# A decode kernel's load order: w_gate first, into a free slot of the key ring, ahead of wq, the first keys and w_up

## The chip, the cores and the metric

One Trainium2 chip, one core. The metric is the device time of one execution in microseconds (us), the median of a few runs: 377.54 us for the kernel before (three runs, 377.37 to 377.6). All tensors are float32. Engines are written as in the profile: PE (TensorE), PEld (its weight loads), DVE (VectorE), ACT (ScalarE), POOL (GpSimd), SP (SyncE, which issues nearly all transfers here).

## What is computed

One token is normalised and goes through two blocks in parallel, attention over a cache of 32 heads x 4096 keys x 128, and a gated feed-forward (FFN) block whose hidden width is 1376:

```
xn = layernorm(x)                                   # 1 x 512
q  = xn @ wq                                        # 32 heads x 128
p  = softmax(q . k_cache * 128**-0.5)               # per head, 4096 keys
A  = (p @ v_cache) @ wo
h  = silu(xn @ w_gate) * (xn @ w_up)                # 1376 wide
B  = xn + (h @ w_down) * sigmoid(xn . w_r)
out = x + A + B
```

The sizes follow from the shapes: wq 8.39 MB, w_gate and w_up 2.82 MB each, k_cache and v_cache 67.1 MB each, wo 8.39 MB, w_down 2.82 MB.

## The kernel before

The 32 heads go in `NG = 8` groups of four. The keys of a group (8.39 MB, 128 partitions x 16384 values) take two of the three slots of `ring` (`SLOT` = 8192 values a partition), the values of a group fill `vals` (two slots wide). The loop at L392 handles, in turn g, the scores of group g and the softmax and the product with the values of group g-1.

- **Keys.** `load_keys` (L99) puts group g into slots 2g mod 3 and the next one, in one transfer, or in two where the ring wraps. K0 takes slots 0 and 1; K1 slot 2 (its first half, here K1a) and slot 0 (K1b); K2 slots 1 and 2.
- **Scores.** DVE multiplies keys by the query (`multiply`, L241) and adds up (`sums`, L251); POOL does the last 24 of 64 rows of each half (`rest`, L256 and L258). The sums of a half free its slot.
- **Softmax.** `own_max` (L304 to L308), `head_max` (L313), `expo` (L321, then POOL L323).
- **Values.** 32 products on PE per group (`values`, L332), two records each in the profile.
- **Queue.** All large transfers are issued by SP, in program order, each behind its own waits. The data then flows in that order.

What stands ahead of the loop matters here. SP loads wq into `vals` (L81) and K0 into the ring (L96). PE makes the query (L217, then L230), ACT copies it (L222, L233). When the products of wq have read the front of `vals`, w_gate and w_up are loaded there (L89, called at L225). DVE and POOL start on K0 (L273 to L275). PE multiplies w_gate into the PSUM bank `ps_acc` and w_up into `ps_o` (`ffn_in`, L261, called at L276). `gate` and `up` are used only after the values of group 0 (`ffn_hidden`, L278). The values of group 0 (V0) overwrite `vals` (L395), so SP waits for the products of w_up.

Of the kernel before, what the change touches and what calls it, by code (L numbers as in the profile page):

```python
# [20 lines left out]
NCOL = 4  # L21
# [6 lines left out]
def kernel(  # L28
# [13 lines left out]
    nc = tc.nc  # L42
    _, H, Sk, Dh = k_cache.shape
    D = x.shape[-1]
    F = w_gate.shape[1]
    NK = D // P
# [10 lines left out]
    FL = F - FM  # L57
    FC = FM // NCOL
    QC = QB * Dh
    HC = C // 2  # L60
    SLOT = HC * Dh
# [15 lines left out]
    ring = const.tile([P, SLOTS * SLOT], F32, name="ring")  # L77
    vals = const.tile([P, 2 * SLOT], F32, name="vals")

    def load_wq(t):  # L80
        nc.sync.dma_start(t, wq.rearrange("(p j) n -> p (j n)", p=P))  # L81

        return [
            t[:, j * H * Dh:(j + 1) * H * Dh].rearrange("p (b h k n) -> p b h k n", b=NB, h=HP, n=QC)
            for j in range(NK)
        ]

    def load_in(t, w):
        nc.sync.dma_start(t, w.rearrange("(p j) f -> p (j f)", p=P))  # L89
        return [t[:, j * F:(j + 1) * F] for j in range(NK)]  # L90
# [8 lines left out]
    def load_keys(g):  # L99

        i = 2 * g % SLOTS * SLOT
        if i + 2 * SLOT <= SLOTS * SLOT:
            t = load_group(k_cache, g, ring[:, i:i + 2 * SLOT])
            return t[:, :HC], t[:, HC:]
        return load_group(k_cache, g, ring[:, i:]), load_group(k_cache, g, ring[:, :SLOT], HC)
# [19 lines left out]
    xr, wr, xn, row = (rows[0:1, i].rearrange("o g d -> o (g d)") for i in range(G))  # L125
    nc.scalar.dma_start(xr, x[0])
    nc.scalar.dma_start(wr, w_r.rearrange("(o n) -> o n", o=1))
    WQ = load_wq(vals)
    K, V = {0: load_keys(0)}, {}

# [8 lines left out]
    ps_acc = ps_1.tile([P, 512], F32, name="ps_acc")  # L139
    ps_o = ps_1.tile([P, 512], F32, name="ps_o")  # L140
# [45 lines left out]
    ps = ps_s.tile([P, 512], F32, name="ps_small")  # L186
    for j in range(NK):
        nc.tensor.matmul(ps[:, j:j + 1], xn.rearrange("o (p j) -> o j p", j=NK)[:, j], ones[0:1, 0:1],  # L188
                         start=True, stop=True)
    xnT = const.tile([P, NK], F32, name="xnT")  # L190
# [13 lines left out]
    ps = ps_s.tile([P, 512], F32, name="ps_small")  # L204
# [5 lines left out]
    nc.vector.tensor_tensor(base, base, xr, op=ALU.add)  # L210


    NR = NQ * HP // NCOL
    for j in range(NK):
        for i in range(NQ * HP):
            t, k = i % NCOL, i // HP
            nc.tensor.matmul(ps_pv[i // NCOL][32 * t:32 * t + 1, :QC], xnT[:, j:j + 1],  # L217
                             WQ[j][:, k * QB // GB, i % HP, k % (GB // QB), :],
                             start=(j == 0), stop=(j == NK - 1), skip_group_check=True)
    q_sb = const.tile([P, NR, QC], F32, name="q_sb")  # L220
    for i in range(NR):
        nc.scalar.activation(q_sb[:, i, :], ps_pv[i][:, :QC], AF.Copy)  # L222


    W_GATE, W_UP = (load_in(vals[:, i * NK * F:(i + 1) * NK * F], w) for i, w in enumerate((w_gate, w_up)))  # L225

    def q_part(k):

        ps = ps_q.tile([P, QB, Dh], F32, name="q")
        nc.tensor.matmul(ps.rearrange("p g d -> p (g d)"), pick.rearrange("p i h -> p (i h)"), q_sb[:, k, :],  # L230
                         start=True, stop=True)

        nc.scalar.activation(q_sb[:, k, :], ps.rearrange("p g d -> p (g d)"), AF.Copy)  # L233
        return ps
# [11 lines left out]
    def sums(g, i):  # L246
        if i == 0:
            S[g] = small.tile([P, C], F32, name="s")
        k, s = K[g][i], S[g][:, i * HC:(i + 1) * HC]
        for c, n in ((slice(0, HC - NP), Dh), (slice(HC - NP, HC), Dh // 2)):  # L250
            nc.vector.tensor_reduce(s[:, c], k[:, c, :n], axis=AX.X, op=ALU.add)  # L251
# [6 lines left out]
        nc.gpsimd.tensor_tensor(a, a, b, op=ALU.add)  # L258


    def ffn_in(W, ps):  # L261

        for j in range(NK):
            for t in range(NCOL):
                a = FL if t else 0
                nc.tensor.matmul(ps[32 * t:32 * t + 1, a:FL + FC], xnT[:, j:j + 1],  # L266
                                 W[j][:, a + t * FC:FL + (t + 1) * FC],
                                 start=(j == 0), stop=(j == NK - 1), skip_group_check=True)
        return ps[:, :FL + FC]

    Q = {0: q_part(0)}

    rest(0, 0)  # L273
    multiply(0, 0, 0, HC - NP)
    sums(0, 0)  # L275
    gate, up = ffn_in(W_GATE, ps_acc), ffn_in(W_UP, ps_o)  # L276

    def ffn_hidden():  # L278

# [112 lines left out]
    for g in range(NG + 1):  # L392
# [3 lines left out]
        elif g:  # L396

            i = 2 * g % SLOTS * SLOT
# [42 lines left out]
    for j in range(NCOL):  # L441
        nc.tensor.matmul(fin(j), ones[0:1, 0:1], base[:, j * DC:(j + 1) * DC],
                         start=True, stop=False, skip_group_check=True)
# [39 lines left out]
```

## Time and profile before

| what | value |
|---|---|
| median of three runs | 377.54 us |
| the profiled execution, its own time | 377.8 us |
| its span, first to last instruction | 375.9 us |
| read from HBM | 159.52 MB, 424 GB/s over the span |
| DMA queue of SP and its packets, share of 16 engines | 98.3% |
| busy share PE / DVE / ACT / POOL | 31% / 61% / 4% / 46% |
| granted PE clock, mean | 0.681 |

The profiled execution took 0.26 us more than the median; its time lies 1.9 us above its span. A "landing" below is the moment at which an engine that waited for a transfer starts. The issue row of a transfer says when SP handed it to the queue, not when its data began to flow.

### The profile page before, as it was taken

What the parts mean: (1) busy time and instruction counts of PE and PEld (TensorE: products, weight loads), DVE (VectorE), ACT (ScalarE), POOL (GpSimd) and SP (SyncE); (2) the same over time, 40 slices, a digit from 0 to 9 for tenths busy, and PEclk for the clock granted to TensorE, in tenths of its full rate; (3) what the DMA queues carried; (4) which work ended last, traced back from release to release, by engine and by line L of the source; (5) the groups of instructions that cost most, each with busy time, mean ns of one, the idle gap of its engine ahead of it and who ended that gap; (6) DMA issues with size and microseconds to landing.
All of it is one profiled execution on the core that took longest, in us unless ns stands there. A gap on an engine that the chain in (4) does not pass through costs nothing.

```text
span 375.9 us, 2047 instructions
## 1 busy us (share of the span) xinstructions
PE 116.5 (31%) x846; PEld 34.4 (9%) x846; DVE 230.8 (61%) x124; ACT 15.6 (4%) x36; POOL 171.5 (46%) x52
## 2 busy tenths in 40 slices
PE   1155063000810072006300580045002700181994
PEld 1111011000200020001100130011000200020222
DVE  6300599999468990799699105994399699500010
ACT  3001000000010000100100000000000000010001
POOL 2000496992008940795696004970399299000000
PEclk9999557555785578555855596559555855586799
DMA  8999899999999899999999899999998999999994
GB/s 335 446 446 446 386 435 443 446 446 446 440 439 425 384 441 446 446 432 398 443 485 425 384 448 446 446 425 441 439 446 387 418 458 439 446 420 404 436 420 199
DMA packets 4190, 159.64 MB, mean 425 GB/s; under 512 B 467, under 2 KB 467, under 8 KB 854
## 3 DMA queue, kind: packets, MB, share of 16 engines
q1 hardware_dynamic: 4178, 159.52, 98.3%
q8 instruction: 6, 0.10, 0.1%
q14 instruction: 2, 0.02, 0.0%
q10 hardware_dynamic: 4, 0.00, 0.0%
HBM read 159.52 MB, written 0.00 MB: 424 GB/s over the span
## 4 chain that ended last, share of the span: by engine, by line
DMA 79%; PE 20%; issue 0%; SPq 0%; ACTq 0%; ACT 0%; DVE 0%
DMA vals<-in_A_v_cache_dram 57%; PE ps_pv L332 17%; DMA ring<-in_A_wo_dram 9%; DMA vals<-in_B_w_up_dram 7%; DMA vals<-in_A_wq_dram 6%; PE ps_pv L217 2%; PE ps_o L266 1%; PE ps_acc L388 0%; SPq L112 0%; PE ps_small L308 0%; ACTq L478 0%; ACT res L451 0%; DVE nm L313 0%; PE ps_o L388 0%
## 5 line engine op out<-in xcount | busy, mean ns | idle before, releaser
L256 POOL TENSOR_TENSOR ring<-ring,q_sb 128x3072 f32<-128x3072 f32 x16 | 106.9, 6679 | 147.3 <-DMA ring<-in_A_k_cache_dram 147.3
L241 DVE TENSOR_TENSOR ring<-ring,q 128x2560 f32<-128x2560 f32 (+1 forms) x23 | 88.7, 3857 | 83.2 <-DMA ring<-in_A_k_cache_dram 83.2
L332 PE MATMUL ps_pv<-vals,pt 128*16 128x512 f32 x448 | 62.5, 721 | 185.6 <-DMA vals<-in_A_v_cache_dram 185.6
L251 DVE TENSOR_REDUCE s<-ring 128x40 f32<-128x5120 f32 (+1 forms) x32 | 114.3, 3614 | 0.8
L258 POOL TENSOR_TENSOR ring<-ring 128x1536 f32<-128x1536 f32 x16 | 55.0, 3435 | 1.3
L332 PEld LDWEIGHTS ps_pv<-vals,pt 128*16 128x16 f32 x448 | 14.9, 111 | 228.3 <-issue 228.3
L323 POOL TENSOR_TENSOR pt<-e,mine 128x512 f32<-128x512 f32 x8 | 8.3, 1042 | 17.7 <-ACT e L321 17.7
L341 ACT ACTIVATE pv<-ps_pv 128x512 f32<-128x512 f32 x8 | 4.8, 597 | 215.0 <-PE ps_pv L332 215.0
L332 PE MATMUL ps_pv<-ring,pt 128*16 128x512 f32 x64 | 9.4, 754 | 10.1 <-DMA ring<-in_A_v_cache_dram 10.1
L357 DVE RECIPROCAL rinv<-ps_small 128x4 f32<-128x4 f32 x2 | 0.4, 178 | 19.7 <-PE ps_small L348 19.7
L217 PE MATMUL ps_pv<-vals,xnT 128*1 128x512 f32 x64 | 9.2, 739 | 10.4 <-DMA vals<-in_A_wq_dram 10.4
L266 PE MATMUL ps_acc<-vals,xnT 128*1 128x320 f32 (+1 forms) x32 | 5.7, 772 | 15.6 <-DMA vals<-in_B_w_gate_dram 15.6
L313 DVE TENSOR_REDUCE nm<-ps_small 128x1 f32<-128x32 f32 x8 | 1.5, 184 | 11.8 <-PE ps_small L308 11.8
L308 PE MATMUL ps_small<-dg,same 128*128 128x32 f32 x16 | 3.6, 309 | 14.5 <-DVE dg L306 14.5
L350 PE MATMUL ps_o<-pv,first 128*128 128x512 f32 x16 | 7.4, 605 | 0.8 <-ACT pv L341 0.8
L321 ACT ACTIVATE e<-s,nm 128x128 f32<-128x128 f32 x8 | 3.2, 402 | 98.4 <-DVE nm L313 98.4
L453 DVE COPY res<-ps_acc 1x128 f32<-1x128 f32 x2 | 0.6, 281 | 10.9 <-PE ps_o L388 10.9
L306 DVE TENSOR_SCALAR dg<-fold,m 128x32 f32<-128x32 f32 x8 | 6.6, 820 | 0.3
L196 DVE TENSOR_SCALAR hid<-hid 128x416 f32<-128x416 f32 x1 | 0.4, 377 | 7.1 <-ACT hid L195 7.1
L308 PEld LDWEIGHTS ps_small<-dg,same 128*128 128x128 f32 x16 | 2.9, 218 | 20.1 <-issue 18.2
L188 PE MATMUL ps_small<-ones,pv 1*128 1x1 f32 x8 | 2.0, 370 | 8.3 <-DVE pv L184 8.3
L359 DVE TENSOR_TENSOR o<-ps_o,rinv 128x512 f32<-128x512 f32 x2 | 2.1, 1064 | 4.0 <-PE ps_o L350 3.9
(88 smaller groups left out, 70.3 us busy)
## 6 DMA issues: line engine op xcount, KB each, us to landing
ring<-in_A_k_cache_dram SPq DMA_DIRECT2D x6, 4096.0 KB, 35.2
vals<-in_A_wo_dram SPq DMA_DIRECT2D x1, 4096.0 KB
vals<-in_B_w_gate_dram SPq DMA_DIRECT2D x1, 2752.0 KB, 20.9
vals<-in_B_w_up_dram SPq DMA_DIRECT2D x1, 2752.0 KB, 25.9
vals<-in_B_w_down_dram SPq DMA_DIRECT2D x1, 2560.0 KB
ring<-in_A_wo_dram SPq DMA_DIRECT2D x1, 2048.0 KB, 31.1
ring<-in_A_wo_dram SPq DMA_DIRECT2D x1, 1024.0 KB, 33.2
ring<-in_A_wo_dram SPq DMA_DIRECT2D x1, 768.0 KB, 34.5
```

Of the source, the lines that this page charges most:

```text
L217: nc.tensor.matmul(ps_pv[i // NCOL][32 * t:32 * t + 1, :QC], xnT[:, j:j + 1], WQ[j][:, k * QB // GB, i % HP, k % (GB // QB), :], start=(j ...
L241: nc.vector.tensor_tensor(k[:, c0:c1, :], k[:, c0:c1, :], q[:, None, :].to_broadcast([P, c1 - c0, Dh]), op=ALU.mult)
L251: nc.vector.tensor_reduce(s[:, c], k[:, c, :n], axis=AX.X, op=ALU.add)
L256: nc.gpsimd.tensor_tensor(k, k, q[:, None, :].to_broadcast([P, NP, Dh]), op=ALU.mult)
L258: nc.gpsimd.tensor_tensor(a, a, b, op=ALU.add)
L266: nc.tensor.matmul(ps[32 * t:32 * t + 1, a:FL + FC], xnT[:, j:j + 1], W[j][:, a + t * FC:FL + (t + 1) * FC], start=(j == 0), stop=(j == NK ...
L306: nc.vector.tensor_scalar(dg, fold, m, SCALE, op0=ALU.mult, op1=ALU.mult)
L308: nc.tensor.matmul(ps[:, :PP], same.rearrange("p i h -> p (i h)"), dg, start=True, stop=True)
L323: nc.gpsimd.tensor_tensor(PT[g % 2], e[:, :, None].to_broadcast([P, C, HP]), mine[:, None, :].to_broadcast([P, C, HP]), op=ALU.mult)
L332: nc.tensor.matmul(ps[r:r + M, :], p[:, G * i:G * (i + 1), :].rearrange("p c h -> p (c h)"), v[:, G * i:G * (i + 1), :].rearrange("p c d - ...
L341: nc.scalar.activation(PV[g // GB][:, :, g % GB, :], ps_pv[g % 2].rearrange("p (c d) -> p c d", c=G), AF.Copy)
L350: nc.tensor.matmul(ps_o, first[:, c].rearrange("p h i -> p (h i)"), pv[:, c].rearrange("p k d -> p (k d)"), start=(c == 0), stop=(c == G - 1))
```

## The change

w_gate is loaded by the first instruction on SP, into slot 2 of the ring, which K1a needs only later. Its products are issued on PE before those of wq. `ffn_in` moves up for that, and w_up alone takes the front of `vals`.

```
+    W_GATE = load_in(ring[:, 2 * SLOT:2 * SLOT + NK * F], w_gate)
     WQ = load_wq(vals)
     K, V = {0: load_keys(0)}, {}
...
+    def ffn_in(W, ps):        # the body is unchanged, moved up from behind rest()
...
+    gate = ffn_in(W_GATE, ps_acc)
     NR = NQ * HP // NCOL
     for j in range(NK):       # the products of wq
...
-    W_GATE, W_UP = (load_in(vals[:, i * NK * F:(i + 1) * NK * F], w) for i, w in enumerate((w_gate, w_up)))
+    W_UP = load_in(vals[:, :NK * F], w_up)
...
     sums(0, 0)
-    gate, up = ffn_in(W_GATE, ps_acc), ffn_in(W_UP, ps_o)
+    up = ffn_in(W_UP, ps_o)
```

How it moves instructions on SP, the issuing engine, at the start of the program (a row is one transfer, destination, source and shape; x2 is two transfers, K1a and K1b). Before:

```order
L81 DMA vals<-in_A_wq_dram 128x16384
L96 DMA ring<-in_A_k_cache_dram 128x1x16384
L89 DMA vals<-in_B_w_gate_dram 128x5504
L89 DMA vals<-in_B_w_up_dram 128x5504
L96 DMA ring<-in_A_k_cache_dram 128x1x8192 x2
L96 DMA vals<-in_A_v_cache_dram 128x1x16384
```

Now:

```order
L89 DMA ring<-in_B_w_gate_dram 128x5504
L81 DMA vals<-in_A_wq_dram 128x16384
L96 DMA ring<-in_A_k_cache_dram 128x1x16384
L89 DMA vals<-in_B_w_up_dram 128x5504
L96 DMA ring<-in_A_k_cache_dram 128x1x8192 x2
L96 DMA vals<-in_A_v_cache_dram 128x1x16384
```

One transfer moved from third place to first, past wq and K0. From w_up on the order is what it was, to the end of the program.

And on PE, at the start of the program (the first rows of w_gate and of wq, the last of wq, the query and what follows). Before:

```order
L205 MATMUL ps_small<-rp,ones 128x1
L217 MATMUL ps_pv_94<-vals,xnT 1x512 x4
...
L217 MATMUL ps_pv_95<-vals,xnT 1x512 x4
L230 MATMUL q<-q_sb,pick 128x512
L266 MATMUL ps_acc<-vals,xnT 1x416
L266 MATMUL ps_acc<-vals,xnT 1x320 x3
...
L266 MATMUL ps_o<-vals,xnT 1x416
```

Now:

```order
L206 MATMUL ps_small<-rp,ones 128x1
L219 MATMUL ps_acc<-ring,xnT 1x416
L219 MATMUL ps_acc<-ring,xnT 1x320 x3
...
L229 MATMUL ps_pv_96<-vals,xnT 1x512 x4
L242 MATMUL q<-q_sb,pick 128x512
L219 MATMUL ps_o<-vals,xnT 1x416
```

The 16 products into `ps_acc` (32 records in the profile) moved from behind the query to ahead of the products of wq. The orders of DVE, ACT and POOL are the same in both kernels.

## Rows read from the trace of the kernel before

**Rows 1.** The page: the span; the shares of the chain that ended last, by engine; two DMA queues with packets, MB and the time of their packets as a share of 16 engines' span.

```profile
span 375.9 us, 2047 instructions
...
q1 hardware_dynamic: 4178, 159.52, 98.3%
q8 instruction: 6, 0.10, 0.1%
...
DMA 79%; PE 20%; issue 0%; SPq 0%; ACTq 0%; ACT 0%; DVE 0%
```

**Rows 2.** The chain of waits in order of time, five of its 81 pieces: start, us, what.

```profile
30.38 25.91 DMA vals<-in_B_w_up_dram
...
56.34 3.02 PE ps_o L266 x28
...
59.37 35.55 DMA vals<-in_A_v_cache_dram
...
104.06 29.48 DMA vals<-in_A_v_cache_dram
...
337.61 34.52 DMA ring<-in_A_wo_dram
```

**Rows 3.** Timeline of SP's queue: start, us, the transfer that was issued. In order: wq, K0, w_gate, w_up, K1a, K1b, V0, K2.

```profile
0.74 0.40 SPq L81 DMA_DIRECT2D vals<-in_A_wq_dram  x1
1.20 0.61 SPq L96 DMA_DIRECT2D ring<-in_A_k_cache_dram  x1
27.82 0.33 SPq L89 DMA_DIRECT2D vals<-in_B_w_gate_dram  x1
30.38 0.33 SPq L89 DMA_DIRECT2D vals<-in_B_w_up_dram  x1
30.76 0.55 SPq L96 DMA_DIRECT2D ring<-in_A_k_cache_dram  x1
...
54.95 0.54 SPq L96 DMA_DIRECT2D ring<-in_A_k_cache_dram  x1
59.37 0.54 SPq L96 DMA_DIRECT2D vals<-in_A_v_cache_dram  x1
...
85.48 0.53 SPq L96 DMA_DIRECT2D ring<-in_A_k_cache_dram  x1
```

**Rows 4.** Timeline of PE up to 70 us: start, us, what, and in brackets the idle time before it and what ended it.

```profile
11.93 0.58 PE L205 MATMUL ps_small<-rp,ones 1*128 1x1 f32 x2 [1.56 <-DVE rp L203]
22.89 9.17 PE L217 MATMUL ps_pv<-vals,xnT 128*1 128x512 f32 x64 [10.38 <-DMA vals<-in_A_wq_dram]
...
48.72 5.71 PE L266 MATMUL ps_acc<-vals,xnT 128*1 128x416 f32 x32 [15.60 <-DMA vals<-in_B_w_gate_dram]
56.34 2.95 PE L266 MATMUL ps_o<-vals,xnT 128*1 128x416 f32 x32 [1.91 <-DMA vals<-in_B_w_up_dram]
```

**Rows 5.** Timeline of DVE from K0's landing to the end of K1's sums, the next instruction after them, and a later instruction of the kind of `dg`.

```profile
42.25 5.49 DVE L241 TENSOR_TENSOR ring<-ring,q 128x5120 f32<-128x5120 f32 x1 [27.86 <-DMA ring<-in_A_k_cache_dram]
47.77 7.15 DVE L251 TENSOR_REDUCE s<-ring 128x40 f32<-128x5120 f32 x2
...
67.53 0.29 DVE L304 TENSOR_REDUCE m<-s 128x1 f32<-128x128 f32 x1
67.85 4.87 DVE L306 TENSOR_SCALAR dg<-fold,m 128x32 f32<-128x32 f32 x1
72.63 2.81 DVE L241 TENSOR_TENSOR ring<-ring,q 128x2560 f32<-128x2560 f32 x1
...
78.30 7.14 DVE L251 TENSOR_REDUCE s<-ring 128x40 f32<-128x5120 f32 x2
...
90.88 7.15 DVE L251 TENSOR_REDUCE s<-ring 128x40 f32<-128x5120 f32 x2
105.10 0.38 DVE L196 TENSOR_SCALAR hid<-hid 128x416 f32<-128x416 f32 x1 [7.08 <-ACT hid L195]
...
110.73 0.24 DVE L306 TENSOR_SCALAR dg<-fold,m 128x32 f32<-128x32 f32 x1
```

**Rows 6.** Timeline of POOL: the first instruction on K0, the last on K0, the first on K1a.

```profile
42.30 6.68 POOL L256 TENSOR_TENSOR ring<-ring,q_sb 128x3072 f32<-128x3072 f32 x1 [39.51 <-DMA ring<-in_A_k_cache_dram]
...
59.27 3.43 POOL L258 TENSOR_TENSOR ring<-ring 128x1536 f32<-128x1536 f32 x1
66.03 6.65 POOL L256 TENSOR_TENSOR ring<-ring,q_sb 128x3072 f32<-128x3072 f32 x1 [3.33 <-DMA ring<-in_A_k_cache_dram]
```

**Rows 7.** Timeline of PEld in the slow first part of the products of wq (start of each four weight loads), and of ACT at the last copy of the query.

```profile
23.70 0.15 PEld L217 LDWEIGHTS ps_pv<-vals,xnT 128*1 128x1 f32 x4 [0.70 <-issue]
24.55 0.15 PEld L217 LDWEIGHTS ps_pv<-vals,xnT 128*1 128x1 f32 x4 [0.70 <-issue]
...
33.16 0.60 ACT L233 ACTIVATE q_sb<-q 128x512 f32<-128x512 f32 x1 [0.42 <-PE q L230]
```

**Rows 8.** Stretches of time: length, busy time of PE, PEld, DVE, ACT, POOL (count), granted PE clock (1.00 is 2.4 GHz, 0.50 is 1.2 GHz), DMA share, GB/s.

```profile
2.00:4.00 2.00, 0.00 (x0) 0.00 (x0) 1.85 (x9) 0.81 (x1) 0.70 (x3) 1.00 0.60 229
4.00:6.00 2.00, 0.00 (x0) 0.00 (x0) 1.83 (x7) 0.00 (x0) 0.00 (x0) 1.00 1.21 524
...
50.00:52.00 2.00, 2.00 (x19) 0.70 (x15) 2.00 (x1) 0.00 (x0) 2.00 (x1) 0.50 1.12 484
...
56.00:58.00 2.00, 1.66 (x26) 0.81 (x30) 2.00 (x1) 0.00 (x0) 2.00 (x1) 1.00 0.87 377
```

More of the change, by code (lines that the diff above doesn't have):

```diff
@@ L127 @@
     nc.scalar.dma_start(wr, w_r.rearrange("(o n) -> o n", o=1))
+    W_GATE = load_in(ring[:, 2 * SLOT:2 * SLOT + NK * F], w_gate)
     WQ = load_wq(vals)
@@ L210, with ffn_in @@
     nc.vector.tensor_tensor(base, base, xr, op=ALU.add)
+    def ffn_in(W, ps):
+        for j in range(NK):
+            for t in range(NCOL):
+                a = FL if t else 0
+                nc.tensor.matmul(ps[32 * t:32 * t + 1, a:FL + FC], xnT[:, j:j + 1],
+                                 W[j][:, a + t * FC:FL + (t + 1) * FC],
+                                 start=(j == 0), stop=(j == NK - 1), skip_group_check=True)
+        return ps[:, :FL + FC]
+    gate = ffn_in(W_GATE, ps_acc)
     NR = NQ * HP // NCOL
@@ L222 @@
         nc.scalar.activation(q_sb[:, i, :], ps_pv[i][:, :QC], AF.Copy)
-    W_GATE, W_UP = (load_in(vals[:, i * NK * F:(i + 1) * NK * F], w) for i, w in enumerate((w_gate, w_up)))
+    W_UP = load_in(vals[:, :NK * F], w_up)
     def q_part(k):
@@ L258, in rest @@
         nc.gpsimd.tensor_tensor(a, a, b, op=ALU.add)
[L261 to L269, printed above, removed]
     Q = {0: q_part(0)}
@@ L275 @@
     sums(0, 0)
-    gate, up = ffn_in(W_GATE, ps_acc), ffn_in(W_UP, ps_o)
+    up = ffn_in(W_UP, ps_o)
     def ffn_hidden():
```

## The prediction

> **What bounds the kernel now.** I read the page first, then the chain of waits, then the timelines of the queue and of the engines that wait for it. The chain puts 79% on DMA and 20% on PE [rows 1], which looks as if products of PE stood between the transfers. Among its pieces are those of w_up, after which V0 is issued [rows 2]. But SP's queue has its packets in flight for 98.3% of the span [rows 1], so such a product can delay the *issue* of a transfer and not its data. The chain shows it: V0 takes 35.55 us from issue to landing and V1 29.48 [rows 2]. V0 was simply issued earlier into a full queue.
>
> So I measured the flow between landings. K0 lands 19.36 us after wq (22.89 to 42.25) [rows 4, 5], 8.39 MB at 433 GB/s. w_gate follows after 6.47 us (to 48.72) [rows 4], 2.82 MB at 436. w_up takes 7.62 (to 56.34), 1.15 more than w_gate for the same bytes. K1a takes 9.69 (to 66.03) [rows 6], 4.19 MB at 433. K1b and V0 take 28.89 (to 59.37 + 35.55 = 94.92) [rows 2], 12.58 MB at 435. K2 and V1 take 38.62 (to 104.06 + 29.48 = 133.54) [rows 2], 16.78 MB at 434. The rate is the same whatever the tensor. The first transfer alone takes 22.89 us where 19.36 would be its flow, so 3.53 us pass at the start. Over the whole kernel: 3.53 + 1.15 + 159.52 MB at 434.5 GB/s (367.1) = 371.8; the last transfer lands at 337.61 + 34.52 = 372.13 [rows 2]. Start, bytes and a tail of 3.8 us make the span. A change of order can only act through the start, or by a gap in the queue.
>
> **The change part by part.** Nothing is added or removed: the same transfers, the same products. Three things move.
>
> *w_gate's transfer goes ahead of wq and K0.* By the flow, w_gate lands at 3.53 + 6.47 = 10.0, wq at 29.36 (6.47 later than before), K0 at 48.72 (6.47 later). w_up then lands at 56.34 and K1a at 66.03 as before, since the bytes ahead of them are the same. The issue of w_gate takes SP 0.33 us [rows 3]; wq and K0 are issued that much later, hidden behind the 6.47 us in which w_gate flows. If the step of 1.15 us that w_up shows comes before K0's end now, K0 lands at 49.87. I carry 48.72 and keep 49.87 as the upper bound.
>
> *w_gate's products go ahead of those of wq.* PE is idle from 12.51 to 22.89 [rows 4], and in the new order until 29.36. 32 records cost 5.71 us at a granted clock of 0.50 (w_gate) or 2.95 at 1.00 (w_up) [rows 4, 8], so they end by 18.3. Queued behind them are the products of wq, due at 29.36: not delayed. K1a, which needs the slot, is issued much later.
>
> *What comes later, and when each would leave the queue dry.* The trace has no transfer issued into an empty queue except the first. That one took 22.15 us from issue (0.74) to landing [rows 3, 4] against 19.36 behind another, so it must be issued at most 2.79 us before its data is due. Zero is the other bound; I take 2.79, the only row there is.
>
> - w_up waits for the front of `vals`, 4.93 us into the products of wq (22.89 to 27.82, where w_gate's issue stands now) [rows 3, 4], so it is issued at 34.3. If PE ran slow throughout (0.85 us for four of 64 loads [rows 7], 6.8 us for that half), 36.2. Due by 48.72 - 2.79 = 45.9. Hidden.
> - The query is ready at 33.76 [rows 7], 10.87 after wq's landing; now 40.2, or 44.7 if all 64 loads go slowly (13.6 instead of 9.17). K0 lands at 48.72. Hidden.
> - **K1b** waits until DVE has the sums of K0's first half: 12.70 us after K0's landing (42.25 to 54.95) [rows 3, 5]. Now 61.42, at most 62.57. Due by 66.03 - 2.79 = 63.24. Before there were 8.3 us to spare; now 1.8, or 0.7. Hidden, but this is where the cover is thin.
> - V0 waits on SP behind K1b, and for the products of w_up. PE will have idled before them, so I cost them at the slow row, 5.71: ready at 62.05. V0's data is due when K1b has flowed, 66.03 + 9.66 = 75.7, so by 72.9. Hidden.
> - **K2** waits for the sums of K1a's half, issued now at 85.48 [rows 3]. DVE's whole turn starts 6.47 later, but part of that is swallowed. `dg` took 4.87 us from 67.85 where a later turn takes 0.24, and ended at 72.72 [rows 5], when POOL's first instruction on K1a ended (66.03 + 6.65 = 72.68) [rows 6]. That instruction had waited 3.33 us for K1a. In the new order POOL ends K0 at 62.70 + 6.47 = 69.17, starts K1a at once and ends that instruction at 75.82. DVE reaches `dg` at 74.3 and leaves it at 75.82, 3.1 late. So K2 is issued at 88.6, or 89.8 with K0's 1.15. Without that overlap it would be 85.48 + 6.47 + 1.15 = 93.1. Due by 94.92 - 2.79 = 92.1. Hidden by 3.5 us.
> - DVE's last sums on K1 end at 98.03 now and DVE then idles 7.08 us [rows 5]. Ending at 101.1 to 102.3 it still meets the next instruction at 105.10. From there on nothing is late.
>
> The page of the Trainium skill "DMA: Bandwidth & Descriptors", section "Latency and other measured facts", gives about 0.6 us to the first byte of a transfer issued by SP. By that the due time of K1b would be near 65.4, an estimate from that figure, with 4.0 us to spare; no run here shows it.
>
> **Sum.** 0 at the start + 0 on PE + 0 for each wait = 0 on the profiled 377.8 us. The runs' median is 0.26 below it, so I forecast 377.5. For the start I keep both ends. If the 2.79 us grew with the size of the first transfer, w_gate would cost a third of it (0.94) and the kernel would gain 1.85. A loss could be one more issue, 0.33. I take 0: in the first 4 us the flow is low (229 GB/s from 2 to 4) and from 4 to 6 it is at 524 [rows 8], so the loss is over before a third of wq has flowed.
>
> **The rivals.**
>
> *B, slower: the queue runs dry at K1b or K2.* wq and K0 come 6.47 us later while K1a and V0 end when they did, so the cover for these two issues shrinks by most of that. For it: 0.7 us is the least margin at K1b. Against: the 2.79 is an upper bound, and the 12.70 us of DVE work do not change. It decides once K1b is issued after 63.24 or K2 after 92.1; each us later is a us at the end. Its price with the worst K2 (93.1) is 1.0: 378.5.
>
> *C, faster: the start shrinks with the first transfer*, by up to 1.85: 375.7. Against it stand the rates of the first windows.
>
> *D, the step of 1.15 us.* Something held w_up's landing and nothing else of its kind. Six packets of another queue, instructions, lie in the span [rows 1], more than there are such steps in the landings I used. If the step is lost in the new order the time is 376.4; if one like it comes on top, 378.7. The page of the Trainium skill "DMA: Bandwidth & Descriptors", section "Why a DMA increments its semaphore by 16 and not by 1", says that a transfer counts as landed when each of up to 16 DMA engines has delivered its share. By that rule one delayed engine holds up every landing behind it once, and a second hold-up adds only if it meets the same engine. The trace agrees in that the later intervals (28.89, 38.62) show no further step.
>
> That the change does not do what it says is no rival: the issue order is SP's program order.
>
> **How the numbers follow.** Forecast (nothing changes) 0.80; B 0.10; C 0.05; D 0.05, half on each side. What a measurement can tell from no change is 0.2%, 0.76 us: faster means under 376.8, slower over 378.3. Faster: C and half of D, 0.075, set at 0.07. Slower: B and half of D, 0.125, set at 0.13. Same: 0.80. The range goes down to 376.8, leaving out C and the lower half of D, and up to 378.5, which takes in B at its price.
>
> **What would show it.** In the profile after: w_gate's products start at about 12.5, wq's at about 29.4, DVE on K0 at 48.7 to 49.9, K1b's issue at 61.4 to 62.6, K2's at 88.6 to 89.8, and V0 and V1 land at 94.9 and 133.5 as before. A V0 landing later than 95.5 with a low GB/s slice between 62 and 68 would show B at K1b, a V1 landing later than 134 with V0 in place B at K2. Landings of wq and K0 each earlier than forecast by the same amount would show C. The prediction is wrong if the last transfer of wo does not land within 0.8 us of 372.1.

## The result: slower, by 0.3 to 0.6%

The changed kernel took 379.79 us (median of 7 runs, 378.11 to 381.18) against 377.45 for the kernel before (7 runs, 377.34 to 377.6): ratio 1.0058, 95% interval 1.0040 to 1.0076. Two later sets of the same kernel gave 378.53 (11 runs, ratio 1.0033, 1.0021 to 1.0045) and 378.50 (8 runs, 1.0030, 1.0019 to 1.0042). The forecast was 377.5 (376.8 to 378.5) and no change. The profiled execution, at 378.13 us with a span of 376.2, is one of the fastest.

SP's queue in the changed kernel (start, us, what was issued: w_gate, wq, K0, w_up, then K1b, V0 and K2; K1a is left out) answers to [rows 3]:

```profile
0.74 0.40 SPq L89 DMA_DIRECT2D ring<-in_B_w_gate_dram  x1
1.19 0.41 SPq L81 DMA_DIRECT2D vals<-in_A_wq_dram  x1
1.66 0.61 SPq L96 DMA_DIRECT2D ring<-in_A_k_cache_dram  x1
34.80 0.34 SPq L89 DMA_DIRECT2D vals<-in_B_w_up_dram  x1
...
62.62 0.54 SPq L96 DMA_DIRECT2D ring<-in_A_k_cache_dram  x1
63.27 0.54 SPq L96 DMA_DIRECT2D vals<-in_A_v_cache_dram  x1
89.75 0.54 SPq L96 DMA_DIRECT2D ring<-in_A_k_cache_dram  x1
```

The engines that wait for these, in timelines of PE, DVE and POOL, answer to [rows 4 to 6]:

```profile
12.45 5.33 PE L219 MATMUL ps_acc<-ring,xnT 128*1 128x416 f32 x32
29.73 9.31 PE L229 MATMUL ps_pv<-vals,xnT 128*1 128x512 f32 x64 [11.95 <-DMA vals<-in_A_wq_dram]
...
56.38 5.55 PE L219 MATMUL ps_o<-vals,xnT 128*1 128x416 f32 x32 [16.28 <-DMA vals<-in_B_w_up_dram]
...
49.93 5.49 DVE L253 TENSOR_TENSOR ring<-ring,q 128x5120 f32<-128x5120 f32 x1 [35.53 <-DMA ring<-in_A_k_cache_dram]
...
75.53 1.46 DVE L308 TENSOR_SCALAR dg<-fold,m 128x32 f32<-128x32 f32 x1
...
70.30 6.65 POOL L268 TENSOR_TENSOR ring<-ring,q_sb 128x3072 f32<-128x3072 f32 x1
```

Nearly every milestone is where the forecast put it: w_gate's products at 12.45, wq at 29.73 (forecast 29.36), K0 at 49.93 (48.7 to 49.9), K2's issue at 89.75 (88.6 to 89.8), and `dg` meets POOL and shrinks to 1.46 us. K1b's issue, 62.62, is at the late end of its range (61.4 to 62.6).

The chain of waits (start, us, what), cut to the pieces from K0 on, answers to [rows 2]:

```profile
1.66 48.18 DMA ring<-in_A_k_cache_dram
...
49.93 5.50 DVE ring L253
...
55.45 7.16 DVE s L263 x2
...
62.62 0.54 SPq L96
...
63.27 31.74 DMA vals<-in_A_v_cache_dram
...
104.25 29.42 DMA vals<-in_A_v_cache_dram
...
142.35 30.54 DMA vals<-in_A_v_cache_dram
...
337.94 34.54 DMA ring<-in_A_wo_dram
```

Before, the chain went from transfer to transfer with products of PE between. Now it runs K0, DVE's multiplication, DVE's sums, SP's issue of K1b, V0: the transfer waits for DVE. Still V0 lands at 63.27 + 31.74 = 95.01, only 0.09 later than before. V1 is 0.13 later (133.67), V2 0.64 (172.89), the last transfer 0.35 (372.48). The loss appears after the place where it arises, which the next view explains.

The stretches from 62 to 70 us and, as the forecast named it, from 62 to 68 (columns as in [rows 8]), first in the kernel before, then in the changed one:

```profile
62.00:70.00 8.00, 0.00 (x0) 0.00 (x0) 7.93 (x4) 0.00 (x0) 4.67 (x2) 0.50 0.96 414
62.00:68.00 6.00, 0.00 (x0) 0.00 (x0) 5.93 (x4) 0.00 (x0) 2.67 (x2) 0.50 1.01 437
```

```profile
62.00:70.00 8.00, 0.00 (x0) 0.00 (x0) 7.96 (x3) 0.00 (x0) 7.92 (x2) 0.69 0.98 397
62.00:68.00 6.00, 0.00 (x0) 0.00 (x0) 5.99 (x2) 0.00 (x0) 5.92 (x2) 0.75 0.90 355
```

The flow is lower, as rival B named it. By how much these rows don't tell, since they count each packet whole in the stretch in which it starts: the kernel before has 414 and 437 with no gap in its packets. With each packet spread over its own length, 62 to 70 us comes to 433 GB/s before and 402 in the changed kernel, which is 0.57 us of flow lost. The packet records of the traces also say on which of the 16 DMA engines. I put consecutive packets together by engine (one starts within some ns of the end of the one before) and read when each engine ended K1a and began K1b, in us:

```
                         K1a ended           K1b's first packet       K1b ended
                       first  mean   last    starts from   length   mean   last
before                 63.81  64.20  65.55       63.80      1.21    73.88  75.23
changed                63.77  64.24  65.62       63.95      1.71    74.49  75.34
change, K0 in two (e2) 63.72  64.16  66.17       63.72      1.21    73.84  75.85
sums thrice (e6)       63.77                     70.30      1.78
```

Fifteen engines end K1a by 65; one ends it at 65.6. On that engine a 16 KB packet of the instruction queue came between two packets of data, and it lost 1.41 us: at 52.8 to 53.8 us in the kernel before, during w_up, and at 38.3 to 39.3 in the changed kernel, during K0. A landing shows the late engine. The others want K1b from 63.8 on, and in the changed kernel their first packet of it took 1.71 us instead of 1.21 (median). So the mean engine ends K1b 0.61 later, the last one only 0.11, and V0's landing hardly moves. The rest comes out when later instruction packets, each again on another engine, hold up engines that are now late (V2).

### The profile page after: what moved, and what is told of

Its sections match the earlier page's. It is cut to its first block, busy times and chain, and to the rows that moved or that the text cites. A ratio compares the mean times of both kernels' runs of the same rounds, so it can differ in the third digit from the quotient of the medians.

```text
span 376.2 us, 2048 instructions
## 1 busy us (share of the span) xinstructions
PE 119.9 (32%) x846; PEld 35.0 (9%) x846; DVE 227.3 (60%) x124; ACT 15.6 (4%) x36; POOL 171.4 (46%) x52
## 4 chain that ended last, share of the span: by engine, by line
DMA 77%; PE 17%; DVE 3%; SPq 1%; issue 0%; ACTq 0%; ACT 0%; DVEq 0%
DMA vals<-in_A_v_cache_dram 55%; PE ps_pv L334 17%; DMA ring<-in_A_k_cache_dram 13%; DMA ring<-in_A_wo_dram 9%; DVE s L263 2%; DVE ring L253 1%; PE ps_acc L390 0%; SPq L112 0%; PE ps_small L310 0%; SPq L96 0%; SPq L81 0%; SPq L89 0%; ACTq L480 0%; ACT res L453 0%; DVE nm L315 0%
## 5 line engine op out<-in xcount | busy, mean ns | idle before, releaser
L334 PE MATMUL ps_pv<-vals,pt 128*16 128x512 f32 x448 | 63.7, 733 | 180.6 <-DMA vals<-in_A_v_cache_dram 180.6
L334 PE MATMUL ps_pv<-ring,pt 128*16 128x512 f32 x64 | 9.4, 750 | 10.2 <-DMA ring<-in_A_v_cache_dram 10.2
L219 PE MATMUL ps_o<-vals,xnT 128*1 128x320 f32 (+1 forms) x32 | 5.6, 770 | 16.3 <-DMA vals<-in_B_w_up_dram 16.3
L219 PE MATMUL ps_acc<-ring,xnT 128*1 128x320 f32 (+1 forms) x32 | 5.3, 759 | 0.0
L334 PEld LDWEIGHTS ps_pv<-ring,pt 128*16 128x16 f32 x64 | 2.2, 114 | 16.6 <-issue 16.6
```

What stands on the lines that cost most here:

```text
L334: nc.tensor.matmul(ps[r:r + M, :], p[:, G * i:G * (i + 1), :].rearrange("p c h -> p (c h)"), v[:, G * i:G * (i + 1), :].rearrange("p c d - ...
```

## The experiments

Theory Q says the queue runs dry at K1b. Its rivals are S, the start with w_gate first is slow, and D (another than rival D of the forecast), any delay of DVE's first turn costs.

**e1, the changed kernel once more**, unedited.

> The changed kernel once more, for a second trace and more times. Theory Q (the queue runs dry at K1b: SP can issue it only at about 62.6, and the engines that are not held up by the 1.15 us step have finished K1a by 63.8): 378 to 381, over 0.2% slower than before, K1b issued at 61.4 to 63.5, and a stretch of low GB/s between 63 and 68. The slower the run, the wider that stretch. Theory S (the first transfer being w_gate makes the start slow and uneven): the slower runs have wq and K0 land later than 29.7 and 49.9, by as much as their time is longer.

378.53 (377.81 to 380.38). K1b issued at 62.41, K0 landed at 49.72, V0 at 95.02; the traced run took 378.31. Nothing in it lands late at the start. S spoke of the slower runs, though, and this is none of them, so it decides little.

**e2, K0 in two transfers** in the changed kernel:

```
-    K, V = {0: load_keys(0)}, {}
+    K, V = {0: (load_group(k_cache, 0, ring[:, :SLOT]), load_group(k_cache, 0, ring[:, SLOT:2 * SLOT], HC))}, {}
```

> The changed kernel, with K0 loaded in two transfers, slot 0 first. DVE can start on the first half when it has landed (about 40) and the query is ready (about 41.7), so slot 0 is free at about 54.4 and K1b is issued there instead of at 62.6. Theory Q: the loss goes, 377.2 to 377.8, and the runs lie within 0.4 us. Theory S: the start is as it was, 378 to 381 with the same spread.

377.59 (11 runs, 377.32 to 378.12), ratio 1.0007 (0.9998 to 1.0016): no difference from before can be measured, with w_gate still first. The runs spread over 0.8 us, twice what was expected. K1b's issue, and the stretch 62 to 70 us:

```profile
53.53 0.54 SPq L96 DMA_DIRECT2D ring<-in_A_k_cache_dram  x1
...
62.00:70.00 8.00, 0.61 (x2) 0.50 (x2) 7.92 (x7) 0.36 (x2) 3.28 (x1) 0.60 0.99 426
```

The issue is 9.1 us earlier, the flow is whole (433 GB/s by the packets' lengths, as before) and the loss is gone. S falls. V0 lands at 95.52 in this trace, later than in the changed kernel, for one engine alone ends late; the mean engine ends K1b 0.04 earlier than before. So a landing of V0 doesn't measure the loss. By itself e2 doesn't tell K1b from K2, which is issued 10.2 us earlier too (79.54); the next runs do.

**e3, e5, e6: K1b delayed in the kernel before**, by repeating DVE work on K0's first half with the same result; the order of transfers stays that of before.

```
e3:      sums(0, 0)
    +    sums(0, 0)
e5: +    nc.vector.tensor_reduce(S[0][:, :HC - NP], K[0][0][:, :HC - NP, :], axis=AX.X, op=ALU.add)
e6: +    sums(0, 0)
    +    sums(0, 0)
```

> The kernel before, with the sums of K0's first half computed twice by DVE (7.15 us more there, the same result), so that K1b is issued at 62.1 instead of 54.95; the order of transfers and products is that of before. Theory Q: like the changed kernel, 377.7 to 381, slower by 0.1 to 0.9%, with runs spread over more than 1 us. Theory S: 377.5, no change, since DVE has 7.08 us to spare later.

> The kernel before, with only the first of the two reduces of K0's first half repeated (5.49 us of DVE, the same result), so that K1b is issued at 60.4. Theory Q with its due time at about 62.2 (the engines that were not held up finish K1a from 63.6 on, and about 1.4 us pass from issue to the first packet): no loss, 377.3 to 377.6, runs within 0.4 us. Theory D (any delay of DVE's first turn costs, through K2 or the later turns, not through K1b): a loss of about three quarters of that of the run with both reduces (0.58), 377.9.

> The kernel before, with the sums of K0's first half computed three times (14.3 us more of DVE), so that K1b is issued at 69.2. Theory Q: the queue is dry from about 63.9 until 70.6, V0 lands 6.5 to 7.5 late, and the time is 383.8 to 385.5: past the due time each us of lateness is a us of the kernel. Theory D: about twice the loss of the run with the sums twice, 378.6.

| K1b issued at | time, us | ratio to before (95%) |
|---|---|---|
| 54.95 (before) | 377.45 beside e3, 377.35 beside e5 and e6 | |
| 60.21 (e5) | 377.50 | 1.0002 (0.9993 to 1.0011) |
| 62.03 (e3) | 378.03 | 1.0019 (1.0010 to 1.0029) |
| 68.97 (e6) | 384.63 | 1.0194 (1.0180 to 1.0208) |

Each kernel's issue row of K1b, e5, e3 and e6 in turn, with that of K2 for e5 and e3, and for e6 the load of V0 and the stretch in which the queue is dry:

```profile
60.21 0.54 SPq L96 DMA_DIRECT2D ring<-in_A_k_cache_dram  x1
...
88.95 0.54 SPq L96 DMA_DIRECT2D ring<-in_A_k_cache_dram  x1
```

```profile
62.03 0.54 SPq L96 DMA_DIRECT2D ring<-in_A_k_cache_dram  x1
...
89.01 0.54 SPq L96 DMA_DIRECT2D ring<-in_A_k_cache_dram  x1
```

```profile
68.97 0.54 SPq L96 DMA_DIRECT2D ring<-in_A_k_cache_dram  x1
...
69.68 31.60 DMA vals<-in_A_v_cache_dram
...
62.00:70.00 8.00, 0.00 (x0) 0.00 (x0) 8.00 (x3) 0.00 (x0) 4.19 (x2) 0.50 0.17 74
```

5.3 us of delay cost nothing that can be measured, 7.1 cost 0.6 us, 14.0 cost 7.3. There is a due time, between 60.2 and 62.0, and past it a us late is about a us lost: from e3 to e6 the issue moves 6.94 us and the time 6.60. D, which has the cost grow with the delay from the start, falls. So does a queue that runs dry at K2: K2 is issued at 88.95 in e5 and at 89.01 in e3, and e3 alone loses. In e6 V0 lands 6.36 us later than before, a little less than Q's 6.5 to 7.5. That the cost appears in a kernel with wq first shows that w_gate's place is not needed for it.

**e4, w_gate second**, in the changed kernel:

```
-    W_GATE = load_in(ring[:, 2 * SLOT:2 * SLOT + NK * F], w_gate)
     WQ = load_wq(vals)
+    W_GATE = load_in(ring[:, 2 * SLOT:2 * SLOT + NK * F], w_gate)
```

> The changed kernel with wq issued first and w_gate second, still into slot 2 and ahead of K0. K0 lands as late as in the changed kernel (48.7 to 49.9), but the first transfer is wq as before. w_gate's products still stand ahead of those of wq on PE, so the query is ready about 6 us later (46.6), still ahead of K0. Theory Q: as slow as the changed kernel, 378 to 381. Theory S: 377.5.

378.27 (377.95 to 378.49), ratio 1.0021 (1.0012 to 1.0029). K0 lands at 49.92, K1b is issued at 62.61. A late K0 without w_gate in first place costs 0.8 us; that agrees with Q and not with S. But no run is over 378.5.

**The tail.** Of the changed kernel's 32 runs, those below included, 12 took over 379 us. Six more of them, r1 to r6, were traced for what makes such a run:

> The changed kernel again, one look, to catch a run of 379.3 us or more with its trace; the two traced so far took 378.13 and 378.31. Theory Q1 (K0 lands late in the slow runs, so K1b is issued late and all engines stand dry for as long): K1b's issue moves past 62.6 by as much as the time grows. Theory Q2 (the restart after the dry moment is what varies, or a second dry moment at K2): K1b is issued at 62.4 to 62.6 and V0 lands late, or V0 lands at 95.0 and V1 late. Theory I (the 1.15 us steps of instruction transfers fall on the same DMA engine twice): landings up to V1 as in the first trace, and a later interval between two landings of values over 39.7 instead of 38.6.

> A further look at the changed kernel, for the same three theories: Q1 late K1b, Q2 late V0 or V1 with K1b at 62.4 to 62.6, I a later interval over 39.7.

> A further look at the changed kernel, for the same three theories: Q1 late K1b, Q2 late V0 or V1 with K1b at 62.4 to 62.6, I a later interval over 39.7.

> The changed kernel again, for a run of 380 us or more; the traces so far reach 379.06. In them the engines lost 0.3 to 0.7 us each at K1b's first packets, and in the slower ones a part of the packets of 64 KB in later stretches took some 0.1 us longer than their 2.42. Theory L (the restart leaves the engines in step, and packets in step are slower): the loss of a slow run lies in many such packets after 70 us, and the intervals between the landings of values exceed 38.7 there. Theory Q2 (the dry moment itself is what varies): it lies in V0's landing.

> As the look before: theory L puts the loss of a slow run in longer intervals between landings after 95 us, theory Q2 in V0's landing.

> As the look before: theory L puts the loss of a slow run in longer intervals between landings after 95 us, theory Q2 in V0's landing.

They took 378.52, 379.06, 378.71, 378.30, 378.11 and 378.35. K1b's issue lies between 62.2 and 62.6 and V0 lands between 94.5 and 95.0 in all six, so neither Q1 nor a varying V0 explains the differences. In r2, the slowest, K1b (62.20), V0 (94.55) and K0 (49.51) are earlier than in the profiled execution, which speaks against S too. In r2 the stretch between the landings of V1 and V2, and the chain's last transfer:

```profile
133.43:173.12 39.69, 10.07 (x68) 2.67 (x69) 25.72 (x11) 1.57 (x4) 21.11 (x6) 0.63 0.98 421
...
338.19 35.30 DMA ring<-in_A_wo_dram
```

From V1's landing to PE's first product with V2 that is 39.69 us; before it took 38.85 (133.54 to 172.39). Theory I's mark, over 39.7, is not reached. The last transfer lands at 373.49, 1.36 later than before. In the packet records of r2, 99 packets that start between 125 and 175 us took 0.03 to 0.3 us longer than the usual 2.42 (64 KB) or 1.21 (32 KB); in the kernel before there are none in that stretch. Spread over 16 engines they make 0.54 us. That is what L expects, but r1 was slow without them (none in that stretch): there the instruction packet at 333.5 to 334.5 met an engine that had lost 0.37 and 0.36 us in two early packets of K1b. In r2 too part of the loss comes at this packet (334.1): the engine that ends last is 0.5 us later than in the kernel before in the transfer ahead of it (327.4) and 1.35 in the next (347.6). Nor do the longer packets need w_gate in first place: counted alike, e3 has 91 of them from 72 to 125 us and e6 91 from 175 to 330, the kernel before 4 in all. No run of 380 us or more has a trace.

Three kernels on one chip were to say whether the tail belongs to w_gate's place. f1 is the changed kernel, f2 that of e4, f3 the changed kernel with `sums(0, 0)` twice, as in e3.

> The changed kernel, beside the next two on one chip. If its tail belongs to w_gate's first place: some of some 11 runs over 379, as in the two sets so far (9 of 18). If the tail was one of sessions: all under 379.

> wq first, w_gate second, K1b as late as in the changed kernel. If the tail belongs to w_gate's first place: 378.0 to 378.5, none over 379, as before. If to the late K1b alone: some runs over 379.

> The changed kernel with the sums of K0's first half computed twice (7.15 us more of DVE), so that K1b is issued at 69.7 and all engines stand empty for some 6 us. The dry time alone gives 384.8 to 385.5, since the run with the sums three times and wq first took 384.63 with K1b at 69.1. If the tail comes from how the engines stand to each other before K1b (some still busy with K1a when K1b is issued), a full stop wipes it out: runs within 1 us. If it comes from something else in w_gate's first place, it stays: runs spread over 2 us or more.

f1: 378.50, 3 of 8 runs over 379. (The two earlier sets had 8 of 18, not 9.) f2: 378.26 (377.91 to 378.58), none of 11. f3: 385.07 (4 runs, 384.80 to 386.08), V0 landing at 101.74. By these counts, 12 of 32 against none of 22 in e4 and f2, the tail goes with w_gate's first place, and only where K1b is late, since e2 has none of 11. The long runs of e3 (up to 378.99) come near it without w_gate first. f3's four runs spread over 1.3 us and decide nothing about a full stop.

## Why the prediction was wrong

- **Where it held.** The reading that only the start or a gap in the queue can move the time stood: e2, with the whole reorder and no gap, takes what the kernel before takes. The moves of w_gate's transfer and products, the query, w_up, V0 and K2, and the swallowing at `dg`, came as forecast. Rival C did not occur: with w_gate first and no gap, e2 gained nothing.
- **The step that failed is K1b, "due by 66.03 - 2.79 = 63.24".** The queue was taken to end with the landing of K1a. That landing is the latest of 16 engines plus the time until the waiting engine starts. The other engines end from 63.8 on. In e6, K1b issued at 68.97, the first packet starts at 70.30, 1.33 us later. So the first engine waits unless K1b is issued by 63.8 - 1.33 = 62.5, not 63.24. Issued at 62.62 it is late. The forecast had what was needed: the 1.15 us of w_up was seen, with one delayed engine as a reading of it, and not taken off the landing of K1a. 63.24 - 1.15 = 62.09 would have put the upper bound of the issue (62.57) past the due time.
- **The lead before that end.** Even 62.5 and 62.09 are not early enough, since e3 loses 0.58 with an issue at 62.03 and e5 nothing at 60.21. 1.33 us is the lead of the engine that starts first: in e3 two engines that had ended K1a at 64.55 and 64.58 began K1b at 64.85 and 65.17, up to 3.1 us after the issue. And first packets are long without a wait: in r2 (issue 62.20) no engine stood still, and 14 of 16 took longer than 1.21. The forecast's 2.79, taken from 63.8 instead of 66.03, gives 61.0, between e5 and e3. So its lead would have done, in part by luck, since it was read from the first transfer; its end of the queue would not.
- **The signs it named.** They would have passed the profiled execution: V0 landed at 95.01, not past 95.5, and the last transfer of wo at 372.48, within 0.8 us of 372.1. Both are landings, and a landing hides 15 late engines behind one that was late already. What gave it away is the low flow between 62 and 68.
- **Which end of K0's range.** I carried 48.72 and kept 49.87 as the bound. The instruction packet came in K0, so the bound was the value (49.84 for K0's landing in the chain).
- **The price.** Rival B said a us for each us late and 1.0 at most, through K2. Being barely late cost more than the lateness: 0.8 us in e4 at 62.61, where the first packets of K1b took about 0.4 us longer (median 1.63), and 0.6 in e3 at 62.03, where most first packets were of the usual length but 91 packets between 72 and 125 us were longer than usual, 0.46 us for each engine. The mean engine of e3 ends K1b 0.13 us later than before and V0 0.62 later; why V0's packets are long there is not shown. B had the mechanism and the place, a chance of 0.10 and a price that was too low. Its condition, an issue after 63.24, was never met; the tail of the changed kernel goes beyond its price.
- **Rival D** had the right suspect. The first instruction packet moved with PE's program, from w_up to K0: it comes after 106 of PE's records in the kernel before and after 102 in the changed one. In these two traces none was lost or met the same engine twice; moving one put K0, and K1b with it, at the late end of its range. Whether an issue at the early end, 61.42, would have been in time no run shows: 60.21 was, 62.03 was not.

The section of the Trainium skill's page "DMA: Bandwidth & Descriptors" on first bytes ("Latency and other measured facts", about 0.6 us) would have had K1b due later still. From the start of its issue e6 measures 1.33 us, from the end of the issue row 0.8; the measurement decides. The rule on that page of the Trainium skill that a transfer lands when its last engine has delivered ("Why a DMA increments its semaphore by 16 and not by 1") agrees with the trace: at K1b the mean engine was 0.61 late and the last one 0.11, and V0's landing was 0.09 late.

What stays open is why w_gate in first place gives a late K1b its tail: the step above accounts for the 0.8 us of e4, not for the 12 runs of the changed kernel that lose 1.6 to 3.7.

## What to carry to other kernels

A queue runs dry at its fastest engine and a landing is that of its slowest: count the cover of an issue from the first engine's end and not from the landing (63.8 and 66.03 here), and leave a lead before that (more than 1.8 us, which was too little in e3; 3.6 was enough in e5). Moving a transfer forward moves back all it passes: the cost lies with whoever waits for those, here the keys whose sums free the slot for the next load. Where such a cover gets thin, split the late transfer, so that work on its first half can start (e2).

## What the runs showed that I had not expected

- Five of the six 16 KB instruction packets in the kernel before each cost one DMA engine 1.41 us, and each a different one. (The sixth comes at the very end.) The end then shows one such step and not five.
- The first packets of a late K1b, 32 KB each, took 1.7 us instead of 1.21, also where the queue had been empty for 6 us (e6, 1.78) and, at 1.56, where no engine had stood still (r2).
